# Weight splits in halves and a planner that holds pieces back: one change to an attention and two-mixture kernel

## The chip, the cores and the metric

The kernel runs on one core of a Trainium2 chip. The core has five engines that work side by side, each through its own queue, in the order of the program: TensorE (PE, with PEld for its weight loads), VectorE (DVE), ScalarE (ACT), GpSimd (POOL) and SyncE (SP), which issues most DMAs. The metric is the time of one execution on the device in microseconds; less is better. Three runs of the kernel before took 769.09, 770.85 and 771.26 us, median 770.85.

## The reference

Three layers follow each other: an attention with decaying state, a mixture of four experts in which every token goes through all of them, and a mixture of eight experts in which each token goes to one.

```python
# attention: chunks of tokens, L = decay between two tokens of a chunk, state carried over
y = ((C @ B.T) * L * causal) @ x + (C @ state) * decay_to_i
state = decay_full * state + sum_j(B_j x_j * decay_from_j)
# first mixture: N = 3072 tokens, D = 256, F = 1024, four experts
out = sum_e p[:, e] * (relu(x @ w1[e]) @ w2[e])
# second mixture: eight experts, each token to the argmax of x @ w_gate, times its softmax weight
out[i] = gate_w[i] * (relu(x[i] @ w1[e_i]) @ w2[e_i])
```

## The kernel before

**Numbers in two parts.** The matmuls take their operands in a reduced form of float32, and precision is kept by splitting every operand into a high part (a copy, on ScalarE) and a low part (the subtraction of the two, on VectorE or GpSimd). One product is then three matmuls: high by high, high by low, low by high (lines 533 to 535 for the first layer of an expert, 562 to 564 for the second). `split_w` (line 402) does this for a quarter of an expert's weights: 128 partitions by 1024 columns. A quarter is called a chunk `c`: 0 and 1 make up `w1`, 2 and 3 `w2`.

**Blocks.** The 3072 tokens are 24 steps of 128. The first mixture goes through them in seven blocks of 2, 3, 4, 4, 4, 4 and 3 steps; a matmul of block 0 has 256 columns, of block 1 384, of blocks 2 to 5 512. In each block each expert has eight slices `f` of its hidden layer. `up(b, e, f)` is a group of six matmuls into a PSUM tile `ph`, after which ScalarE writes `hh` = relu (line 538) and VectorE `hl`, the low part (line 539). `down(b, e, f)` is six matmuls from `hh` and `hl` into the accumulators `acc`. `down` runs two slices behind `up` (LAG = 2), so PE's order is `up f`, `down f-2`, `up f+1`, `down f-1` and so on. There are two `ph` buffers: `up f+2` needs `hl` of `f` to be done. There are three buffers for accumulators, and an expert uses two; after its last slice, `combine` multiplies them by the token's weight on VectorE (lines 578 and 583). The opening expert of block 0 (expert 0) is different: its raw weights are multiplied in full float32, one step of 128 tokens after the other (lines 516 and 552, `ph32`), since its weights are not split yet.

**Attention beside it.** While PE goes through a block of the first mixture, the attention of the next block's steps is put in between, in pieces. Per step: `decay` (two scans on VectorE, 128 x 512, tile `lt`, line 181), `prefix` (a scan `pre` and the product `cd`), `low` and `high` (packing of keys and queries into `bp` and `cbd`, lines 206 and 202), `scores` (PE, tiles `sc`, in PSUM), `mask` (two multiplications `m0` and `m1` on VectorE, line 247, `sc` by `lt`), `state_in` (`bw`), `products` (PE: `y` from the state, line 255; the new state, line 291; `y` from the masked scores, line 263: the first half of it reads `m0`, the second `m1`), then `split` (ScalarE's `xh`, VectorE's `xl`) and `state`. The PSUM tiles `sc` and `y` share three buffers: `y` of heads 4 to 7 takes the buffer of `sc0`, and so needs `m0` to be done. `USUAL` and `FIRST` (lines 318 and 321) list which pieces stand together.

**What sets the order.** The order on all engines is that in which the program issues the instructions. `tick` (line 998) is called once after each `up` and once after each `down`; its calls are counted as slots. A slot issues first what a table `wq` has for it (weight splits, loads), then a piece of the routing of the block before, then as many attention pieces as keep them spread evenly over the block. The table at lines 969 to 973 sets the slots in which VectorE splits the first mixture's weights: those of experts 1, 2 and 3 in block 0, and of expert 0 in block 1. Each such split is one ScalarE copy (line 408) and one VectorE subtraction of 1024 columns (line 409). The second mixture's preparation (`part_split`, line 372) has its subtractions already in halves.

Of the kernel before, what the change touches and what calls it, by code (L numbers as in the profile page):

```python
# [17 lines left out]
P = 128  # L18
# [7 lines left out]
FF = 1024  # L26
NF = FF // P
# [9 lines left out]
BLOCKS = [2, 3, 4, 4, 4, 4, 3]  # L37
# [32 lines left out]
def attention_moe_moe_kernel(ctx: ExitStack, tc: tile.TileContext, aps: dict, cap: int):  # L70
    nc = tc.nc
# [90 lines left out]
    def attention_pieces(s, xH, xL, col):  # L162
# [238 lines left out]

    def split_w(moe, e, c, lo):
        if (moe, e) not in W:
            W[moe, e] = weights(moe, e)
        h, l = W[moe, e][2 * (c // 2):2 * (c // 2) + 2]
        sl = slice(FF * (c % 2), FF * (c % 2) + FF)
        st = given[moe, e, c]
        nc.scalar.copy(h[:, sl], st)
        lo.tensor_tensor(l[:, sl], st, h[:, sl].bitcast(F32), ALU.subtract)
# [71 lines left out]
    def block_attention(b):  # L481
        new_xT(b)
        r = []
        for i in range(BLOCKS[b]):
            d = attention_pieces(starts[b] + i, *xT[b], P * i)
            for group in FIRST if starts[b] + i < OPENING else USUAL:
                r.append(lambda fns=[d[k[:-1]][int(k[-1])] for k in group]: [fn() for fn in fns])
        return r

    hid, acc, pb = {}, {}, {}  # L490
# [450 lines left out]
    urgent, side, done = [], [], 0  # L941
    fills = fill_pieces()
    wq = {}

    def at_slot(b, i, fn):
        wq.setdefault((b, i), []).append(fn)

# [21 lines left out]
    for b, i, e, c in (  # L969
# [3 lines left out]
        at_slot(b, i, lambda e=e, c=c: split_w(1, e, c, nc.vector))  # L973
    for i, e, c in ((19, 2, 0), (20, 2, 1), (21, 2, 2), (22, 2, 3), (30, 3, 0), (31, 3, 1), (36, 3, 2), (37, 3, 3)):
# [3 lines left out]
    for i in range(len(apart)):  # L978
        b, s = 2 + i // 3, 16 * (i % 3)
        at_slot(b, s + 2, lambda i=i: part_load(i))  # L980
        at_slot(b, s + 20, lambda i=i: part_split(i, 0))
        at_slot(b, s + 24, lambda i=i: part_split(i, 1))
        at_slot(b, s + 27, lambda i=i: part_store(i))
# [11 lines left out]

    slot = 0

    def tick(b):
        nonlocal slot, done
        nslot = 2 * sum(v[0] == b for v in seq)  # L1000
        for fn in wq.get((b, slot), []):
            fn()
        if b == 1 and fills and slot % 3 == 2:
            fills.pop(0)()
        if b == 1 and slot == nslot - 1:
            while fills:
                fills.pop(0)()
        if urgent:
            urgent.pop(0)()
        wait = 11 if b == 0 else 4  # L1010
        while done < len(side) and done < math.ceil((slot + 1 - wait) * len(side) / (nslot - 6 - wait)):
            side[done]()
            done += 1
        slot += 1

    for i in range(len(seq) + LAG):
        if i < len(seq):
            b, e, f = seq[i]
            if e == experts(b)[0] and f == 0:
                while done < len(side):  # L1020
                    side[done]()
                    done += 1
# [3 lines left out]
                side = block_attention(b + 1) if b + 1 < len(BLOCKS) else []  # L1026
                done, slot = 0, 0
            up(b, e, f)
            tick(b)
        if i >= LAG:  # L1030
# [193 lines left out]
```

## Time and profile before

| | |
|---|---|
| time, median of three runs | 770.85 us |
| the profiled execution | 771.84 us |
| its span, first to last instruction | 770.1 us |
| TensorE | 759.5 us busy, 4746 matmuls |
| VectorE | 444.6 us busy, 892 instructions |
| ScalarE | 286.3 us busy, 589 instructions |
| GpSimd | 159.3 us busy |
| TensorE's granted clock | 0.998 of full speed |

How to read it: matmuls overlap in the record, so that TensorE can be counted busy through a short wait. A wait is seen better as a step between the starts of two matmuls that is longer than others of the same shape. On VectorE and ScalarE too an instruction starts a little before the end of the one in front of it, so that what it costs the queue is the step to the next start, and what a reader of its result waits for is its end.

Times in the profile count from the start of the span. Block 0 lasts from about 14 to 75 us, block 1 from there to about 150 us.

### The profile page before, as it was taken

The page shows a single profiled execution, that of the slowest core. Times are in us where ns is not written, and L with a number is a line of the kernel's source. Part 1 is how long each engine was busy: PE and PEld are TensorE (multiplying, and loading weights), DVE is VectorE, ACT ScalarE, POOL GpSimd, SP SyncE. Part 2 cuts the span into 40 slices and gives each one's busy share as a digit, 9 for nine tenths or more (in the row PEclk, how much of TensorE's full clock was granted, in tenths as well). Part 3 has the DMA queues.
Part 4 walks back from the last instruction along what each step waited for, and adds up shares of the span by engine and source line. Part 5 has one row for each costly group of instructions (what it writes and reads, how often), then busy time and mean ns, then how long its engine had stood idle before and what let it go on. Part 6 is the DMA issues. An engine that isn't in the chain of part 4 may idle for free. (4 is left out here: it accounts for less than half of the span.)

```text
span 770.1 us, 12919 instructions
## 1 busy us (share of the span) xinstructions
PE 759.5 (99%) x4746; PEld 666.5 (87%) x4746; DVE 444.6 (58%) x892; ACT 286.3 (37%) x589; POOL 159.3 (21%) x217
## 2 busy tenths in 40 slices
PE   9999999999999999999999999999999999999996
PEld 7899999988887888878888888888999999999996
DVE  5786778467663686636766356563343444556432
ACT  1552443233332333323333233222345334545432
POOL 1010102212210222101221023110286411111211
PEclk9999999999999999999999999999999999999999
DMA  9763567832433325333253312403053324667100
GB/s 255 233 209 110 186 197 223 231 111 86 162 127 124 113 78 176 127 123 110 80 174 127 123 59 69 142 14 134 15 188 124 93 68 180 233 208 256 56 25 29
DMA packets 55957, 103.50 MB, mean 134 GB/s; under 512 B 5745, under 2 KB 35650, under 8 KB 55869
## 3 DMA queue, kind: packets, MB, share of 16 engines
q1 hardware_dynamic: 52100, 95.48, 38.5%
q0 software_dynamic: 2400, 6.11, 2.2%
q10 hardware_dynamic: 1368, 0.81, 0.5%
q8 instruction: 47, 0.77, 0.4%
q14 instruction: 42, 0.34, 0.1%
HBM read 76.05 MB, written 26.80 MB: 134 GB/s over the span
## 5 line engine op out<-in xcount | busy, mean ns | idle before, releaser
L539 DVE SCALAR_TENSOR_TENSOR hl<-ph,hh 128x512 fp32r<-128x512 f32 (+2 forms) x216 | 133.8, 620 | 220.1 <-ACT hh L538 218.0
L538 ACT ACTIVATE hh<-ph 128x512 fp32r<-128x512 f32 (+2 forms) x216 | 117.4, 543 | 334.0 <-PE ph L535 323.5
L533 PE MATMUL ph<-xh,w1h 128*128 128x512 f32 (+2 forms) x432 | 160.6, 372 | 0.7 <-DVE hl L539 0.7
L562 PE MATMUL acc<-hh,w 128*128 128x512 f32 (+2 forms) x432 | 158.0, 366 | 0.6 <-DVE x L578 0.5
L534 PE MATMUL ph<-xl,w1h 128*128 128x512 f32 (+2 forms) x432 | 156.5, 362 | 0.0
L535 PE MATMUL ph<-xh,w1l 128*128 128x512 f32 (+2 forms) x432 | 156.4, 362 | 0.0
L563 PE MATMUL acc<-hl,w 128*128 128x512 f32 (+2 forms) x432 | 156.3, 362 | 0.0
L564 PE MATMUL acc<-hh,w 128*128 128x512 f32 (+2 forms) x432 | 156.1, 361 | 0.0
L562 PEld LDWEIGHTS acc<-hh,w 128*128 128x128 f32 x432 | 81.2, 188 | 13.0 <-issue 1.4
L533 PEld LDWEIGHTS ph<-xh,w1h 128*128 128x128 f32 x432 | 81.2, 188 | 12.6 <-issue 2.4
L535 PEld LDWEIGHTS ph<-xh,w1l 128*128 128x128 f32 x432 | 81.2, 188 | 10.5
L564 PEld LDWEIGHTS acc<-hh,w 128*128 128x128 f32 x432 | 81.3, 188 | 10.4
L563 PEld LDWEIGHTS acc<-hl,w 128*128 128x128 f32 x432 | 81.3, 188 | 9.4
L534 PEld LDWEIGHTS ph<-xl,w1h 128*128 128x128 f32 x432 | 81.3, 188 | 8.6
L586 POOL TENSOR_TENSOR x<-x,cmb 128x512 f32<-128x512 f32 (+2 forms) x40 | 48.5, 1233 | 150.0 <-DVE cmb L583 150.0
L778 PE MATMUL yy<-w,ring_hh 128*128 128x512 f32 x208 | 76.3, 398 | 0.0
L767 DVE SCALAR_TENSOR_TENSOR ring_hl<-qh,ring_hh 128x384 fp32r<-128x384 f32 (+2 forms) x77 | 36.5, 477 | 55.6 <-ACT ring_hh L766 52.2
L766 ACT ACTIVATE ring_hh<-qh 128x384 fp32r<-128x384 f32 (+2 forms) x77 | 33.0, 428 | 72.2 <-PE qh L764 67.7
L779 PE MATMUL yy<-w,ring_hl 128*128 128x256 f32 x208 | 58.3, 280 | 0.0
L181 DVE TENSOR_TENSOR_SCAN lt<-abc,id 128x512 f32<-128x512 f32 x44 | 56.6, 1287 | 0.0
L778 PEld LDWEIGHTS yy<-w,ring_hh 128*128 128x128 f32 x208 | 39.1, 188 | 6.1
L809 POOL DMA_INDIRECT out<-yo,gi x26 | 25.5, 979 | 78.6 <-DVE yo L808 75.1
(173 smaller groups left out, 991.8 us busy)
## 6 DMA issues: line engine op xcount, KB each, us to landing
stg<-in_w SPq DMA_DIRECT2D x24, 512.0 KB, 3.6
abc<-a_zero SPq DMA_DIRECT2D x21, 512.0 KB, 4.4
bcr<-in_bc SPq DMA_DIRECT2D x19, 512.0 KB, 3.7
disp<-zrow SPq DMA_DIRECT2D x12, 516.0 KB, 8.2
nat<-in_nat SPq DMA_DIRECT2D x24, 256.0 KB, 4.1
raw<-in_w SPq DMA_DIRECT2D x10, 512.0 KB
parts<-high SPq DMA_DIRECT2D x10, 512.0 KB, 3.5
parts<-raw SPq DMA_DIRECT2D x10, 512.0 KB, 3.5
```

Source lines behind the costliest of these rows:

```text
L181: nc.vector.tensor_tensor_scan(t["lt"][:, sl, :].rearrange("p h i -> p (h i)"), a_bc[:, sl, :].rearrange("p h i -> p (h i)"), id4.rearrang ...
L533: nc.tensor.matmul(ph[:, :n], lhsT=wh[:, c], rhs=xh[:, k, :n], start=k == 0, stop=False)
L534: nc.tensor.matmul(ph[:, :n], lhsT=wh[:, c], rhs=xl[:, k, :n], start=False, stop=False)
L535: nc.tensor.matmul(ph[:, :n], lhsT=wl[:, c], rhs=xh[:, k, :n], start=False, stop=k == KD - 1)
L538: nc.scalar.activation(hh[:, :n], ph[:, :n], AF.Relu)
L539: nc.vector.scalar_tensor_tensor(hl[:, :n], ph[:, :n], 0.0, hh[:, :n].bitcast(F32), ALU.max, ALU.subtract)
L562: nc.tensor.matmul(a[:, :n], lhsT=wh[:, c], rhs=hh[:, :n], start=f == 0, stop=False)
L563: nc.tensor.matmul(a[:, :n], lhsT=wh[:, c], rhs=hl[:, :n], start=False, stop=False)
L564: nc.tensor.matmul(a[:, :n], lhsT=wl[:, c], rhs=hh[:, :n], start=False, stop=f == NF - 1)
L586: (nc.vector if (b, e) == (last, experts(b)[-1]) else nc.gpsimd).tensor_tensor(dst[d], dst[d], tmp[d], ALU.add)
L778: nc.tensor.matmul(y, lhsT=hh[:, q], rhs=w2[:, :, c], start=j == 0, stop=False)
L779: nc.tensor.matmul(y[:, 0], lhsT=hl[:, q], rhs=w2[:, 0, c], start=False, stop=j == NF - 1)
```

## The change

A split of a first-mixture chunk on VectorE becomes two instructions of 512 columns, one in each of two slots that follow each other; ScalarE's copy stays whole and goes with the first. The slots are moved: some chunks of experts 1 to 3 come one to eight slots later. And `tick` keeps an estimate `queue` of VectorE's outstanding work, in ns, which falls by `span` with each slot and rises by the load of what is issued. An attention piece with a load in the table `LOAD` (scans, masks, low packs, `state_in`, and the casts and the state update at the end) is held back while the estimate would pass 1.6 slots, until it is three pieces behind its turn (one in the last quarter of a block). Pieces with no load, `scores` and `products` among them, are not held themselves, but they wait for those in front of them in the list. Two helper functions are new: `columns`, the estimate of an instruction, and the changed `at_slot`, which takes a load.

```diff
+    LOAD = dict(
+        prefix0=640, decay0=1280, decay1=1280, low0=640, low1=640, low2=640, mask0=640, mask1=640, state_in0=320,
+        split1=512, state0=448)
...
-    def split_w(moe, e, c, lo):
+    def split_w(moe, e, c, lo, part=None):
...
-        nc.scalar.copy(h[:, sl], st)
+        if part != 1:
+            nc.scalar.copy(h[:, sl], st)
+        if part is not None:
+            half = slice(FF // 2 * part, FF // 2 * part + FF // 2)
+            h, l, st = h[:, sl][:, half], l[:, sl][:, half], st[:, half]
+            sl = slice(None)
         lo.tensor_tensor(l[:, sl], st, h[:, sl].bitcast(F32), ALU.subtract)
...
+    def columns(n):
+        return n * 5 // 4 + 96
...
-            (0, 13, 1, 0), (0, 16, 1, 1), (0, 20, 1, 2), (0, 24, 1, 3), (0, 34, 2, 0), (0, 37, 2, 1), (0, 41, 2, 2),
+            (0, 13, 1, 0), (0, 16, 1, 1), (0, 21, 1, 2), (0, 28, 1, 3), (0, 34, 2, 0), (0, 37, 2, 1), (0, 43, 2, 2),
...
-        at_slot(b, i, lambda e=e, c=c: split_w(1, e, c, nc.vector))
+        for part in range(2):
+            at_slot(b, i + part, lambda e=e, c=c, part=part: split_w(1, e, c, nc.vector, part), columns(FF // 2))
...
+        span = 6 * columns(P * BLOCKS[b]) // 3 if slot >= 4 * NF or b else columns(2 * P)
+        queue = max(0, queue - span) + own
+        for load, fn in wq.get((b, slot), []):
+            queue += load
             fn()
...
-        while done < len(side) and done < math.ceil((slot + 1 - wait) * len(side) / (nslot - 6 - wait)):
-            side[done]()
+        while done < len(side):
+            ahead_of = (slot + 1 - wait) * len(side) / (nslot - 6 - wait) - done
+            load = side[done][0]
+            if ahead_of <= 0 or ahead_of < (3 if 4 * slot < 3 * nslot else 1) and load and queue + load > 8 * span // 5:
+                break
+            queue += load
+            side[done][1]()
             done += 1
...
-            tick(b)
+            tick(b, columns(P * BLOCKS[b]) if (b, e) != (0, 0) else 0)
```

How it moves instructions is shown at three places; names carry the step or the block, expert and slice (`m02` is mask 0 of step 2, `hl0_1_0` the low part of block 0, expert 1, slice 0, `w2_1_1` the split `w2` of expert 1).

VectorE's queue before, from the first scan of step 2 to the first `hl` of expert 1, while the opening expert ends:

```order
L181 SCALAR_TENSOR_TENSOR lt2_338<-abc2_137,id4_87 128x512
L409 TENSOR_TENSOR w1l_1_1_344<-early_w1l_106,w1h_1_1_343 128x1024 x2
L181 SCALAR_TENSOR_TENSOR lt2_338<-abc2_137,id4_87 128x512
L282 TENSOR_TENSOR bw2_389<-nat2_216,lt2_338 128x128
L409 TENSOR_TENSOR w2_1_1_345<-early_w2_104,w2_1_1_345 128x1024
L247 TENSOR_TENSOR m02_402<-sc2_0_362,lt2_338 128x512
L247 TENSOR_TENSOR m12_412<-sc2_1_363,lt2_338 128x512
L409 TENSOR_TENSOR w2_1_1_345<-early_w2_104,w2_1_1_345 128x1024
L936 TENSOR_TENSOR xl0_100<-spare0_101,xh0_99 128x2x256
L539 SCALAR_TENSOR_TENSOR hl0_1_0_474<-ph0_1_0_466,hh0_1_0_473 128x256
```

The same stretch of VectorE's queue after the change:

```order
L417 TENSOR_TENSOR w1l_1_1_342<-early_w1l_106,w1h_1_1_341 128x512 x4
L181 SCALAR_TENSOR_TENSOR lt2_364<-abc2_137,id4_87 128x512
L417 TENSOR_TENSOR w2_1_1_343<-early_w2_104,w2_1_1_343 128x512
L181 SCALAR_TENSOR_TENSOR lt2_364<-abc2_137,id4_87 128x512
L417 TENSOR_TENSOR w2_1_1_343<-early_w2_104,w2_1_1_343 128x512
L282 TENSOR_TENSOR bw2_416<-nat2_216,lt2_364 128x128
L949 TENSOR_TENSOR xl0_100<-spare0_101,xh0_99 128x2x256
L247 TENSOR_TENSOR m02_429<-sc2_0_385,lt2_364 128x512
L417 TENSOR_TENSOR w2_1_1_343<-early_w2_104,w2_1_1_343 128x512
L247 TENSOR_TENSOR m12_445<-sc2_1_386,lt2_364 128x512
L417 TENSOR_TENSOR w2_1_1_343<-early_w2_104,w2_1_1_343 128x512
L552 SCALAR_TENSOR_TENSOR hl0_1_0_478<-ph0_1_0_470,hh0_1_0_477 128x256
```

The masks `m02` and `m12` stood in front of the last chunk's split and of `xl0`; now `xl0`, which needs a cast by ScalarE, stands in front of both, and a half of the last chunk in front of `m12`. On PE the products of step 2 come two groups of four matmul records later (after `ph32_1_7`, before after `ph32_1_6`).

VectorE's queue before, around the masks of step 3, while expert 1 of block 0 ends:

```order
L282 TENSOR_TENSOR bw3_605<-nat3_384,lt3_510 128x128
L409 TENSOR_TENSOR w2_1_2_525<-spare3_103,w2_1_2_525 128x1024
L539 SCALAR_TENSOR_TENSOR hl0_1_6_623<-ph0_1_6_615,hh0_1_6_622 128x256
L247 TENSOR_TENSOR m03_629<-sc3_0_559,lt3_510 128x512
L539 SCALAR_TENSOR_TENSOR hl0_1_7_645<-ph0_1_7_637,hh0_1_7_644 128x256
L247 TENSOR_TENSOR m13_648<-sc3_1_560,lt3_510 128x512
L409 TENSOR_TENSOR w2_1_2_525<-spare3_103,w2_1_2_525 128x1024
L539 SCALAR_TENSOR_TENSOR hl0_2_0_666<-ph0_2_0_658,hh0_2_0_665 128x256
L539 SCALAR_TENSOR_TENSOR hl0_2_1_701<-ph0_2_1_693,hh0_2_1_700 128x256
L583 TENSOR_TENSOR cmb0_1_0_710<-acc0_1_0_528,pb0_1_477 128x256
L583 TENSOR_TENSOR cmb0_1_1_712<-acc0_1_1_529,pb0_1_477 128x256
```

The same stretch after the change:

```order
L417 TENSOR_TENSOR w2_1_2_516<-spare3_103,w2_1_2_516 128x512
L282 TENSOR_TENSOR bw3_657<-nat3_400,lt3_574 128x128
L552 SCALAR_TENSOR_TENSOR hl0_2_0_667<-ph0_2_0_659,hh0_2_0_666 128x256
L417 TENSOR_TENSOR w2_1_2_516<-spare3_103,w2_1_2_516 128x512
L247 TENSOR_TENSOR m03_678<-sc3_0_613,lt3_574 128x512
L552 SCALAR_TENSOR_TENSOR hl0_2_1_688<-ph0_2_1_680,hh0_2_1_687 128x256
L417 TENSOR_TENSOR w2_1_2_516<-spare3_103,w2_1_2_516 128x512
L596 TENSOR_TENSOR cmb0_1_0_698<-acc0_1_0_519,pb0_1_481 128x256
L596 TENSOR_TENSOR cmb0_1_1_700<-acc0_1_1_520,pb0_1_481 128x256
L247 TENSOR_TENSOR m13_704<-sc3_1_614,lt3_574 128x512
L552 SCALAR_TENSOR_TENSOR hl0_2_2_734<-ph0_2_2_726,hh0_2_2_733 128x256
```

Both masks stood in front of the second split of `w2_1_2` and of the two combines `cmb`; now `m13` is behind both halves of it and both combines.

PE's queue before, around the products of step 3:

```order
L562 MATMUL acc0_1_1_529<-hh0_1_6_622,w2_1_1_345 128x256
L563 MATMUL acc0_1_1_529<-hl0_1_6_623,w2_1_1_345 128x256
L564 MATMUL acc0_1_1_529<-hh0_1_6_622,w2_1_1_345 128x256
L255 MATMUL y3_0_675<-cd3_501,state_85 64x128 x2
L255 MATMUL y3_1_676<-cd3_501,state_85 64x128 x2
L291 MATMUL y3_1_676<-nat3_384,bw3_605 32x64 x4
L263 MATMUL y3_0_675<-m03_629,nat3_384 32x128 x4
L263 MATMUL y3_1_676<-m13_648,nat3_384 32x128 x4
L533 MATMUL ph0_2_1_693<-xh0_99,w1h_1_2_523 128x256
```

PE's queue after the change, at the same products:

```order
L575 MATMUL acc0_1_1_520<-hh0_1_7_646,w2_1_1_343 128x256
L576 MATMUL acc0_1_1_520<-hl0_1_7_647,w2_1_1_343 128x256
L577 MATMUL acc0_1_1_520<-hh0_1_7_646,w2_1_1_343 128x256
L255 MATMUL y3_0_706<-cd3_558,state_85 64x128 x2
L255 MATMUL y3_1_707<-cd3_558,state_85 64x128 x2
L291 MATMUL y3_1_707<-nat3_400,bw3_657 32x64 x4
L263 MATMUL y3_0_706<-m03_678,nat3_400 32x128 x4
L263 MATMUL y3_1_707<-m13_704,nat3_400 32x128 x4
L546 MATMUL ph0_2_2_726<-xh0_99,w1h_1_2_514 128x256
```

The products, which read `m13` last, follow slice 7 of expert 1's `down` (before slice 6), which is what the combines read, with no group between.

VectorE's queue before, around mask 1 of step 6 in block 1:

```order
L539 SCALAR_TENSOR_TENSOR hl1_2_4_1409<-ph1_2_4_1401,hh1_2_4_1408 128x384
L247 TENSOR_TENSOR m06_1412<-sc6_0_1398,lt6_1389 128x512
L181 SCALAR_TENSOR_TENSOR lt6_1389<-abc6_1214,id4_87 128x512
L539 SCALAR_TENSOR_TENSOR hl1_2_5_1436<-ph1_2_5_1428,hh1_2_5_1435 128x384
L247 TENSOR_TENSOR m16_1446<-sc6_1_1423,lt6_1389 128x512
L539 SCALAR_TENSOR_TENSOR hl1_2_6_1456<-ph1_2_6_1448,hh1_2_6_1455 128x384
```

The same stretch after the change:

```order
L552 SCALAR_TENSOR_TENSOR hl1_2_4_1418<-ph1_2_4_1410,hh1_2_4_1417 128x384
L181 SCALAR_TENSOR_TENSOR lt6_1421<-abc6_1255,id4_87 128x512
L247 TENSOR_TENSOR m06_1432<-sc6_0_1423,lt6_1421 128x512
L552 SCALAR_TENSOR_TENSOR hl1_2_5_1442<-ph1_2_5_1434,hh1_2_5_1441 128x384
L181 SCALAR_TENSOR_TENSOR lt6_1421<-abc6_1255,id4_87 128x512
L552 SCALAR_TENSOR_TENSOR hl1_2_6_1468<-ph1_2_6_1460,hh1_2_6_1467 128x384
L247 TENSOR_TENSOR m16_1471<-sc6_1_1455,lt6_1421 128x512
```

`m16` stood in front of `hl1_2_6` and now stands behind it. PE's `up` of slice 6, which `hl1_2_6` reads, comes right before the products of step 6 in both kernels.

From block 2 on the order of PE differs only in that the second scores of steps 12, 16 and 20 come one `down` later, and that of VectorE in single low packs and scans that move by an instruction or a few.

## Rows read from the trace of the kernel before

**Rows 1.** The page's first part: busy time of each engine, share, instructions.

```profile
PE 759.5 (99%) x4746; PEld 666.5 (87%) x4746; DVE 444.6 (58%) x892; ACT 286.3 (37%) x589; POOL 159.3 (21%) x217
```

**Rows 2.** View of waits, PE: engine, line, releaser, us in total, times, longest.

```profile
PE ph L533 <- DVE hl L539: 0.7, 2, 0.4
```

**Rows 3.** Timeline, PE, steps at the waits: start, us, what, [idle before, releaser].

```profile
36.68 0.28 PE L563 MATMUL acc<-hl,w 128*128 128x256 f32 x1
36.80 0.28 PE L564 MATMUL acc<-hh,w 128*128 128x256 f32 x1
37.57 0.38 PE L562 MATMUL acc<-hh,w 128*128 128x256 f32 x1 [0.49 <-DVE x L578]
37.79 0.28 PE L563 MATMUL acc<-hl,w 128*128 128x256 f32 x1
...
56.76 0.28 PE L564 MATMUL acc<-hh,w 128*128 128x256 f32 x1
57.47 0.39 PE L533 MATMUL ph<-xh,w1h 128*128 128x256 f32 x1 [0.43 <-DVE hl L539]
...
101.48 0.33 PE L563 MATMUL acc<-hl,w 128*128 128x384 f32 x1
101.66 0.34 PE L564 MATMUL acc<-hh,w 128*128 128x384 f32 x1
102.22 0.47 PE L229 MATMUL sc<-cbd,bp 128*128 128x256 f32 x2 [0.23 <-DVE cbd L206]
```

**Rows 4.** Timeline, PE, around the products of step 2.

```profile
29.44 0.61 PE L552 MATMUL acc<-h,early_w1h 128*128 128x128 f32 x4
29.89 0.61 PE L516 MATMUL ph<-spare,stg 128*128 128x128 f32 x4
30.43 0.43 PE L255 MATMUL y<-cd,state 32*64 32x128 f32 x4
31.04 0.43 PE L255 MATMUL y<-cd,state 32*64 32x128 f32 x4 [0.18 <-DVE m L247]
...
31.54 0.62 PE L263 MATMUL y<-m,nat 128*32 128x128 f32 x16
32.09 0.71 PE L552 MATMUL acc<-h,early_w1h 128*128 128x128 f32 x4
...
34.24 0.61 PE L552 MATMUL acc<-h,early_w1h 128*128 128x128 f32 x4
```

**Rows 5.** Timeline, DVE, the same stretch.

```profile
30.30 1.28 DVE L247 TENSOR_TENSOR m<-sc,lt 128x512 f32<-128x512 f32 x2
31.50 1.21 DVE L409 TENSOR_TENSOR w<-early_w,w 128x1024 fp32r<-128x1024 f32 x1
32.63 0.68 DVE L936 TENSOR_TENSOR xl<-spare,xh 128x512 fp32r<-128x512 f32 x1
34.92 0.42 DVE L539 SCALAR_TENSOR_TENSOR hl<-ph,hh 128x256 fp32r<-128x256 f32 x1 [1.60 <-ACT hh L538]
35.26 0.48 DVE L275 TENSOR_TENSOR xl<-y,xh 128x128 fp32r<-128x128 f32 x2
...
36.10 0.42 DVE L539 SCALAR_TENSOR_TENSOR hl<-ph,hh 128x256 fp32r<-128x256 f32 x1
```

**Rows 6.** Timeline, ACT, the same stretch.

```profile
29.88 1.04 ACT L408 CAST w<-early_w 128x1024 fp32r<-128x1024 f32 x1
...
30.98 0.62 ACT L935 CAST xh<-spare 128x512 fp32r<-128x512 f32 x1
33.34 0.28 ACT L519 ACTIVATE h<-ph 128x128 f32<-128x128 f32 x1 [1.75 <-PE ph L516]
```

**Rows 7.** Timeline, DVE, the first combine of expert 1.

```profile
50.84 0.74 DVE L583 TENSOR_TENSOR cmb<-acc,pb 128x256 f32<-128x256 f32 x2
```

**Rows 8.** Timeline of PE and DVE, the products of step 6.

```profile
108.51 0.62 PE L263 MATMUL y<-m,nat 128*32 128x128 f32 x16
...
109.00 0.56 DVE L539 SCALAR_TENSOR_TENSOR hl<-ph,hh 128x384 fp32r<-128x384 f32 x1 [0.93 <-ACT hh L538]
```

More of the change, by code (lines that the diff above doesn't have):

```diff
@@ L486, in block_attention @@
             for group in FIRST if starts[b] + i < OPENING else USUAL:
-                r.append(lambda fns=[d[k[:-1]][int(k[-1])] for k in group]: [fn() for fn in fns])
-        return r
+                r.append((
+                    sum(LOAD.get(k, 0) for k in group),
+                    lambda fns=[d[k[:-1]][int(k[-1])] for k in group]: [fn() for fn in fns]))
+        return r
+    def columns(n):
+        return n * 5 // 4 + 96
     hid, acc, pb = {}, {}, {}
@@ L943, in attention_moe_moe_kernel, with at_slot @@
     wq = {}
-    def at_slot(b, i, fn):
-        wq.setdefault((b, i), []).append(fn)
+    def at_slot(b, i, fn, load=0):
+        wq.setdefault((b, i), []).append((load, fn))
     def split_at(b, slots, moe, e, engines=(nc.gpsimd,) * 4):
@@ L980, in attention_moe_moe_kernel @@
         at_slot(b, s + 2, lambda i=i: part_load(i))
-        at_slot(b, s + 20, lambda i=i: part_split(i, 0))
-        at_slot(b, s + 24, lambda i=i: part_split(i, 1))
+        at_slot(b, s + 20, lambda i=i: part_split(i, 0), columns(FF // 2))
+        at_slot(b, s + 24, lambda i=i: part_split(i, 1), columns(FF // 2))
         at_slot(b, s + 27, lambda i=i: part_store(i))
@@ L994, in attention_moe_moe_kernel, with tick @@
     at_slot(last, 48, lambda: turned(0, 0))
-    slot = 0
-    def tick(b):
-        nonlocal slot, done
+    slot = queue = 0
+    def tick(b, own=0):
+        nonlocal slot, done, queue
         nslot = 2 * sum(v[0] == b for v in seq)
-        for fn in wq.get((b, slot), []):
+        span = 6 * columns(P * BLOCKS[b]) // 3 if slot >= 4 * NF or b else columns(2 * P)
+        queue = max(0, queue - span) + own
+        for load, fn in wq.get((b, slot), []):
+            queue += load
             fn()
@@ L1020, in attention_moe_moe_kernel @@
                 while done < len(side):
-                    side[done]()
+                    side[done][1]()
                     done += 1
@@ L1039, in attention_moe_moe_kernel @@
             if i < len(seq):
-                tick(b)
+                tick(b, 2 * columns(P * BLOCKS[bb]) if ff == NF - 1 else 0)
     ahead = [(0, k) for k in range(1, min(nblk, 2))] + [(1, 0)]
```

2 rows, old and new, of the table steps1 are left out of this document.

## Prediction, made before the changed kernel was run

> **What bounds the kernel now.** I read the page's first part first: TensorE (PE) is counted busy for 759.5 of 770.1 us, VectorE (DVE) for 444.6 [rows 1]. A busy PE hides short waits, because matmuls overlap in the record, so I then read the view of waits for PE and the timeline of PE where it names VectorE. The reader is to see two things. First, the step from one matmul to the next is regular (0.12 us for 256 columns, 0.18 for 384 [rows 3]), and exceptions are few. Second, the view of waits charges PE little to VectorE (0.7 us in two waits to the `hl` subtractions [rows 2]), and the rows of these waits lie where VectorE also splits the first mixture's weights [rows 3]. The time is therefore PE's work plus PE's waits. PE's work is not changed, so every microsecond of this change is a wait removed or added on PE.
>
> The waits that can go [rows 3]: from 36.80 to 37.57 PE stood for 0.77 - 0.12 = 0.65 us behind the combine of the opening expert, and the step after it took 0.22 in place of 0.12, since the next weights had not been loaded ahead; 0.75 in all. At 56.76 it was 0.71 - 0.12 = 0.59 and 0.10 again, 0.7; there is a second wait of this kind (both together are 0.7 in the view of waits [rows 2]), which I take at 0.45. At 101.66 it was 0.56 - 0.18 = 0.4 behind the low half of `cbd`, and 0.1 after it. Sum 2.4 us. This is all that the change can win from the waits it reorders; other short ones keep their order.
>
> **The change part by part.** *Halves.* 16 subtractions of 1024 columns become 32 of 512. A whole one goes on after 1.13 us (31.50 to 32.63); one of 512 columns of the same kind takes 0.68 and two in a row go on every 0.60 [rows 5]. So each split costs VectorE 2 x 0.60 - 1.13 = 0.07 us more, 1.1 us in all, beside an engine that is idle four tenths of the time: nothing by itself. The ScalarE copy in front is not halved: 1.04 us [rows 6], and the first half waits for all of it.
>
> *Held pieces.* The estimate delays scans, masks and low packs by up to three pieces, but the products have no load in the table, so they go as soon as their turn comes, now close behind the masks. What PE waits for is then decided by what stands in front of the mask in VectorE's queue. I follow the queue at the places that the order shows.
>
> Step 2 (third chunk, during the opening expert). The products stand two groups later on PE: `ph32_1_6` starts at 29.89, each group takes 0.45 (29.44 to 29.89), so PE is there at 29.89 + 3 x 0.45 = 31.25, about 31.3 [rows 4]. On VectorE mask 0 now stands behind `xl0`, which needs ScalarE's cast, done at 30.98 + 0.62 = 31.6 [rows 6]. So `xl0` at 31.6, mask 0 from 32.2 to 32.9. The second half of the state product, which takes mask 0's PSUM buffer, would come 0.61 - 0.18 = 0.43 after the first (30.43 to 31.04, less the wait in the row's bracket), at 31.75, and waits until 32.95: 1.2 us. In front of mask 1 stands a half of the last weight chunk; its ScalarE copy now comes after the last Relu (0.28), so it ends at 31.6 + 0.28 + 1.04 = 32.9, the half at 33.5, mask 1 at 34.2. The weighted products' second half would come at 32.95 + 0.50 + 0.28 = 33.75 (31.04 to 31.54, and half of 31.54 to 32.09) and waits 0.5. Together 1.7 us; before, the same place waited 0.18 [rows 4]. Net +1.5. Behind mask 1 on VectorE are a half and the first `hl`, which wait for PE anyway. Bounds: +1.1, if the copy overlaps so that only `xl0` holds PE, and +2.0.
>
> The combine's wait then goes: it no longer stands behind the casts, the state update and the scan of the next step. -0.75.
>
> The sixth `up` of expert 1 (`ph0_1_5`) must wait until `hl0_1_3` has read its PSUM buffer. With u the end of `ph0_1_2`: `hl0_1_2` starts at u + 0.68 (34.24 to 34.92 [rows 4, 5]), ScalarE's copy ends at u + 1.7, two halves at 2.9, the casts and the state at 2.9 + 0.84 (35.26 to 36.10) = 3.75, `hl0_1_3` at 4.2. PE has five groups of 6 x 0.12 = 0.72 before it, 3.6, because the scores that stood between are moved away. Wait 0.6, and 0.1 after it: +0.7. Bounds 0.3 and 1.1, by when ScalarE starts the copy.
>
> Step 3. With u the end of `ph0_2_0`: ScalarE's copy of the last chunk ends at u + 1.7, its first half at 2.3, mask 0 at 2.95. PE is at the products after three groups, 2.16 + 0.1, and at the second half of the state product, 0.43 on, at 2.7: waits 0.3. It would be at mask 1 at 3.0 + 0.78 = 3.8. VectorE meanwhile goes on from 2.9 with `hl0_2_1` (0.34), the second half (0.60), the two combines (0.74 [rows 7]), and ends mask 1 (0.68) at 5.2. Wait 1.4. Sum +1.7. The combines read what PE ends just ahead of the products, and the half (0.60) and `hl` (0.34) alone are 0.9 in front of them: bounds 0.9 and 2.4.
>
> The two waits on `hl` (1.15) go: halves stand alternately with `hl`, 0.94 us in a period of 1.44.
>
> Block 1. The low `cbd` of step 6 has a whole `up` group more: -0.5. But step 6's mask 1 now stands behind `hl1_2_6`, which needs the `up` group right in front of the products on PE. Before, this `hl` started at 109.00 as soon as it could; it goes on after about 0.48 of its 0.56, so mask 1 is done at 109.5 + 0.68 = 110.2, where PE was at 108.51 + 0.28 = 108.8 [rows 8]. Wait 1.4, and no luck in the queue can shorten it: bounds 1.3 and 1.6. In step 5 the same flip has one down group more (6 x 0.18 = 1.05): 0.2, between 0 and 0.4.
>
> Blocks 2 to 4. Low packs of steps 10, 14 and 18 move behind an `hl` and a half split, still a full group ahead of their scores: 0.3 for all, between 0 and 0.8 (one 0.60 too late and a little). SP's queue: step 3's decay load goes behind three weight loads, but its scan too stands some 6 us later; nothing.
>
> **Sum.** +1.5 - 0.75 + 0.7 + 1.7 - 1.15 - 0.5 + 1.4 + 0.2 + 0.3 = +3.4 us. The profiled execution took 771.84 us (span 770.1 and 1.7 around it), so 775.2; it lay 1.0 above the median of the runs, 770.85, so I forecast 774.3.
>
> **The rivals.** *B, the waits that it was made for go and nothing comes in their place*: 771.84 - 2.4 = 769.4, against the median 768.45, -0.31%, faster. It decides wherever masks are done before PE arrives, that is if VectorE's queue ahead of them is at most one `hl`. For it: VectorE is idle four tenths of the time and PE's waits are all on it. [...] Against it: step 6's mask cannot start before an `hl` that did not start before 109.00, whatever the queue.
>
> *C, the new waits come at their lower ends*: 1.1 + 0.3 + 0.9 + 1.3 - 2.4 = +1.2, 772.05 against the median, within 0.3%. For it: each PE wait also gives VectorE and ScalarE time to catch up, so a later wait shrinks by part of an earlier one; I let only the waits on the combine and on `hl` profit. Against it: in steps 2, 3 and 6 the queue in front of the mask hangs on PE's own last group, and moves with it.
>
> *D, the stalls cascade*: PE's delay in block 0 puts off everything on ScalarE too, and a late copy holds later `hl`s: upper ends, 2.0 + 1.1 + 2.4 + 1.6 + 0.4 + 0.8 - 2.0 = +6.3, 777.15. For it: ScalarE's copies stay whole and in line with the Relus. Against it: behind step 3's products VectorE has room in each period, 0.94 of 1.44.
>
> *E, the change doesn't do what it says* (the hold never acts): the order excludes it.
>
> **How the numbers follow.** About 0.3%, 2.3 us, is what a measurement of this kernel can tell from no change. Forecast (+2.3 to +5.0) 0.56, D 0.1, C (-2.3 to +2.3) 0.24, B 0.1. Slower 0.66, same 0.24, faster 0.1. The range goes from 770.8, which leaves B and the lowest part of C out, to 777.0: 0.8 of the chance. The forecast's own range is 773.2 to 775.9.
>
> **What would show it.** In the profile after: PE's view of waits names the masks (`m`, the line of the mask's multiplication) several times with waits over 0.5 us, with PE standing at about 31.7 and in the products of steps 3 and 6; the waits on the combine at 37 us and on `hl` at 57 us are gone; PE's times after 150 us are those of before, moved by a constant. Step 6 is the surest: if PE does not wait over a microsecond for `m` there, my reading of the order is wrong. If PE reaches the end of block 0 (the first 384-column `up`) no later than before, the terms of steps 2 and 3 were wrong, and the forecast with them.

## The result and the profile after

The changed kernel took 777.0 us (median of 6 runs, 775.86 to 778.15) against 770.82 us of the kernel before (6 runs, 769.09 to 771.26): the ratio is 1.0082, with a 95% interval of 1.0068 to 1.0096. It is slower by 6.2 us where 3.4 were forecast: 777.0 is the upper end of the range, and +6.2 is just past the +6.15 (777.0 less 770.85) that the range allowed. The profiled execution took 775.86 us, span 774.1.

The first part of the page after, TensorE's (PE's) line. Its busy time is still 759.5 us [rows 1]; the span is 4.0 us longer:

```profile
PE 759.5 (98%) x4746; PEld 666.1 (86%) x4746; DVE 446.1 (58%) x908; ACT 286.6 (37%) x589; POOL 157.2 (20%) x217
```

The view of waits of PE, after (us in total, times, longest). It answers to [rows 2]: the masks `m` take 4.2 us where they took 0.4, POOL's product `bw` appears, and one wait on `hl` is left, at another place:

```profile
PE y L263 <- DVE m L247: 2.5, 4, 1.2
PE y L255 <- DVE m L247: 1.7, 3, 1.0
...
PE y L291 <- POOL bw L282: 0.8, 2, 0.6
PE ph L546 <- DVE hl L552: 0.7, 1, 0.7
...
PE sc L229 <- DVE cbd L206: 0.2, 1, 0.2
```

The masks in the same view before:

```profile
PE y L263 <- DVE m L247: 0.2, 1, 0.2
PE y L255 <- DVE m L247: 0.2, 1, 0.2
```

PE's timeline after (start, us, line, operation; the bracket is the idle time before and what ended it), at the products of step 2, the sixth `up` of expert 1, the products of steps 3 and 5, and the products of step 6:

```profile
30.74 0.43 PE L255 MATMUL y<-cd,state 32*64 32x128 f32 x4
32.18 0.43 PE L255 MATMUL y<-cd,state 32*64 32x128 f32 x4 [1.00 <-DVE m L247]
...
33.50 0.43 PE L263 MATMUL y<-m,nat 128*32 128x128 f32 x8 [0.42 <-DVE m L247]
...
40.97 0.28 PE L577 MATMUL acc<-hh,w 128*128 128x256 f32 x1
41.93 0.39 PE L546 MATMUL ph<-xh,w1h 128*128 128x256 f32 x1 [0.68 <-DVE hl L552]
...
51.49 0.43 PE L255 MATMUL y<-cd,state 32*64 32x128 f32 x4 [0.31 <-DVE m L247]
...
53.59 0.43 PE L263 MATMUL y<-m,nat 128*32 128x128 f32 x8 [1.20 <-DVE m L247]
...
95.11 0.43 PE L255 MATMUL y<-cd,state 32*64 32x128 f32 x4 [0.37 <-DVE m L247]
...
111.26 0.32 PE L291 MATMUL y<-nat,bw 128*32 128x64 f32 x8 [0.58 <-POOL bw L282]
...
112.46 0.43 PE L263 MATMUL y<-m,nat 128*32 128x128 f32 x8 [0.66 <-DVE m L247]
```

VectorE's timeline after, at the same places. At step 2, mask 0 (31.44) stands behind `xl0`, mask 1 (32.76) behind a half. At 39.40 two halves and the casts stand ahead of the `hl` at 41.46. At step 3, mask 1 (52.85) stands behind a half and two combines. At step 6, the second scan (109.45) and then an `hl` stand ahead of mask 1 (111.72):

```profile
30.83 0.69 DVE L949 TENSOR_TENSOR xl<-spare,xh 128x512 fp32r<-128x512 f32 x1 [0.40 <-ACT xh L948]
31.44 0.69 DVE L247 TENSOR_TENSOR m<-sc,lt 128x512 f32<-128x512 f32 x1
32.15 0.69 DVE L417 TENSOR_TENSOR w<-early_w,w 128x512 fp32r<-128x512 f32 x1
32.76 0.68 DVE L247 TENSOR_TENSOR m<-sc,lt 128x512 f32<-128x512 f32 x1
...
39.40 1.29 DVE L417 TENSOR_TENSOR w1l<-early_w,w1h 128x512 fp32r<-128x512 f32 x2 [0.51 <-ACT w1h L412]
40.61 0.48 DVE L275 TENSOR_TENSOR xl<-y,xh 128x128 fp32r<-128x128 f32 x2
...
41.46 0.42 DVE L552 SCALAR_TENSOR_TENSOR hl<-ph,hh 128x256 fp32r<-128x256 f32 x1
...
51.59 0.68 DVE L417 TENSOR_TENSOR w<-spare,w 128x512 fp32r<-128x512 f32 x1
52.18 0.75 DVE L596 TENSOR_TENSOR cmb<-acc,pb 128x256 f32<-128x256 f32 x2
52.85 0.69 DVE L247 TENSOR_TENSOR m<-sc,lt 128x512 f32<-128x512 f32 x1
...
109.45 1.22 DVE L181 TENSOR_TENSOR_SCAN lt<-abc,id 128x512 f32<-128x512 f32 x1
111.25 0.56 DVE L552 SCALAR_TENSOR_TENSOR hl<-ph,hh 128x384 fp32r<-128x384 f32 x1 [0.58 <-ACT hh L551]
111.72 0.68 DVE L247 TENSOR_TENSOR m<-sc,lt 128x512 f32<-128x512 f32 x1
```

The two profiles are compared best from PE's first product on, since the start before it differs from execution to execution (two profiles of the changed kernel have that product at 13.77 and 14.65 us). PE's timeline of the kernel before: the first product of the opening expert, the first `up` matmul with 384 columns (the end of block 0 on PE) and the last one:

```profile
14.35 1.16 PE L516 MATMUL ph<-spare,stg 128*128 128x128 f32 x8 [0.17 <-ACT spare L188]
...
74.52 0.34 PE L533 MATMUL ph<-xh,w1h 128*128 128x384 f32 x1
...
601.00 0.33 PE L533 MATMUL ph<-xh,w1h 128*128 128x384 f32 x1
```

The same three of the changed kernel:

```profile
13.77 1.16 PE L529 MATMUL ph<-spare,stg 128*128 128x128 f32 x8 [0.17 <-ACT spare L188]
...
76.70 0.34 PE L546 MATMUL ph<-xh,w1h 128*128 128x384 f32 x1
...
605.49 0.33 PE L546 MATMUL ph<-xh,w1h 128*128 128x384 f32 x1
```

Block 0 took 74.52 - 14.35 = 60.17 us and takes 76.70 - 13.77 = 62.93, +2.76. From there to the last `up` it took 526.48 and takes 528.79, +2.31. Together the change adds 5.07 us of waiting; the changed profile happened to start 0.58 earlier and to be 0.46 shorter behind the last `up`, which leaves the 4.0 between the profiles.

### The profile page after: what moved, and what is told of

Same layout as the page of the kernel before. It is cut to its first block, busy times and chain, and to the rows that moved or that the text cites. A ratio compares the mean times of both kernels' runs of the same rounds, so it can differ in the third digit from the quotient of the medians.

```text
span 774.1 us, 12941 instructions
## 1 busy us (share of the span) xinstructions
PE 759.5 (98%) x4746; PEld 666.1 (86%) x4746; DVE 446.1 (58%) x908; ACT 286.6 (37%) x589; POOL 157.2 (20%) x217
## 5 line engine op out<-in xcount | busy, mean ns | idle before, releaser
L599 POOL TENSOR_TENSOR x<-x,cmb 128x512 f32<-128x512 f32 (+2 forms) x40 | 44.8, 1142 | 170.0 <-DVE cmb L596 169.9
L780 DVE SCALAR_TENSOR_TENSOR ring_hl<-qh,ring_hh 128x384 fp32r<-128x384 f32 (+2 forms) x77 | 36.8, 477 | 56.6 <-ACT ring_hh L779 55.5
L181 DVE TENSOR_TENSOR_SCAN lt<-abc,id 128x512 f32<-128x512 f32 x44 | 54.6, 1240 | 0.0
```

The lines of the kernel that those rows point to most:

```text
L181: nc.vector.tensor_tensor_scan(t["lt"][:, sl, :].rearrange("p h i -> p (h i)"), a_bc[:, sl, :].rearrange("p h i -> p (h i)"), id4.rearrang ...
L599: (nc.vector if (b, e) == (last, experts(b)[-1]) else nc.gpsimd).tensor_tensor(dst[d], dst[d], tmp[d], ALU.add)
```

## The experiments

"Slots" are the calls of `tick`. Each run was timed beside the kernel before, whose median is given with it. The last table puts all profiles side by side.

**Run 1: the changed kernel again.** No edit.

> The changed kernel itself once more, to see what of the 6 us between the medians is in the program. Theory of the added waits (the mask waits and what follows them are all of it): 4.5 to 5 us over the kernel before when the two traces are counted from the first product of the opening expert on, and every profile of the changed kernel shows the same waits; the rest of the 6 us is the first 14 us, where the profiled execution of the changed kernel happened to be 0.6 us early. Rival (a second cost, later in the program): another execution of the changed kernel shows a wait of 1 us or more behind 40 us that the first profile does not have.

Measured: 776.72 us against 771.68, ratio 1.0075 (1.0057 to 1.0094). The execution that was profiled took 779.51, and all mask waits stand in it as in the first profile. Its 3.65 us over the first profile lie nearly all in three places: 0.88 ahead of the first product (14.65 against 13.77), 1.51 in block 0, and 1.16 behind the last `up`, where the trace shows one matmul of the second mixture 0.9 us late, at 704.55 us. That late matmul is not the change's: the profiles of runs 2, 3, 4 and 12 show it too. The 1.51 in block 0 do not come from longer waits. The windows of run 1 just behind the waits of step 2 (busy times, then the granted clock, DMA share and GB/s) show PE busy at a granted clock of 0.50:

```profile
34.00:35.00 1.00, 0.61 (x9) 0.23 (x9) 0.93 (x2) 0.27 (x1) 0.00 (x0) 0.68 0.75 151
35.00:36.00 1.00, 1.00 (x9) 1.00 (x6) 0.00 (x0) 0.27 (x1) 0.00 (x0) 0.50 1.11 221
36.00:37.00 1.00, 1.00 (x6) 1.00 (x6) 0.00 (x0) 0.00 (x0) 0.00 (x0) 0.50 0.96 229
37.00:38.00 1.00, 1.00 (x8) 1.00 (x7) 0.01 (x1) 0.38 (x1) 0.00 (x0) 0.62 1.03 309
```

The same stretch in the first profile of the same program:

```profile
35.00:36.00 1.00, 1.00 (x11) 1.00 (x10) 0.20 (x1) 0.38 (x1) 0.00 (x0) 1.00 1.03 295
36.00:37.00 1.00, 1.00 (x11) 1.00 (x10) 0.26 (x2) 0.38 (x1) 0.00 (x0) 1.00 1.10 303
```

At 0.50 the step from one matmul of 256 columns to the next was 0.21 us (36.21 to 36.42 in run 1), at 1.00 it was 0.12 (35.81 to 35.93 in the first profile). Ahead of this stretch PE stood 1.00 and 0.42 us for the two masks of step 2, in both profiles. So the first theory holds for the waits, and there is a further cost that it had no term for: in some executions the clock falls behind them, here to 0.50.

**Run 2: halves, nothing held back.**

```diff
-            if ahead_of <= 0 or ahead_of < (3 if ...) and load and queue + load > 8 * span // 5:
+            if ahead_of <= 0:
```

> The halves at their new places stay; nothing is held back, so pieces of attention go at the slots they had before. Theory (holding back makes the waits, halves are nearly free): 769 to 771 us; no wait for a mask over 0.3 us in steps 2, 3 and 6; the waits for the hl subtractions at 55 and 57 us smaller than before. Rival (the halves are the cost: twice the instructions, the last part of each chunk later): 774 to 777 us, with waits on hl or on the weights in block 0.

Measured: 771.84 us against 771.68, ratio 1.0005 (0.9991 to 1.0020). The median lies just above the 769 to 771 that was expected, and it is that of the kernel before within its interval: the halves and their new places cost nothing and win nothing that can be measured. The two waits on `hl` at 55 and 57 us are gone from the trace, but the combine's wait at 36 us is 1.0 us over the usual step, a new one on an `hl` at 34.9 us is 0.4, and one on a mask of step 2 is 0.56, more than the 0.3 expected. Holding back makes the loss. In this trace the halves ended two waits, lengthened another and made new ones, with no gain in time.

**Run 3: holding back, whole splits at the old places.**

```diff
-        for part in range(2):
-            at_slot(b, i + part, lambda ...: split_w(1, e, c, nc.vector, part), columns(FF // 2))
+        at_slot(b, i, lambda e=e, c=c: split_w(1, e, c, nc.vector), columns(FF))
```

The table of slots goes back with it.

> Whole splits at the places of before, with the holding back kept (its estimate of the queue gets the load of a whole split). Theory (holding back makes the waits): 774 to 777 us, the mask waits of steps 2, 3 and 6 as in the changed kernel: over 1 us for step 6, over 1 us for step 2. Rival (halves are the cost): 769 to 772 us.

Measured: 776.73 us against 771.68, ratio 1.0066 (1.0045 to 1.0087). Step 2's second half of the state product stands 1.9 us for its mask, step 6 0.6 for `bw` and 0.6 for mask 1. PE's granted clock is 0.50 from 34 to 40 us. Holding back alone is as slow as the whole change.

**Run 4: masks not held back.**

```diff
-        prefix0=640, ..., mask0=640, mask1=640, state_in0=320,
+        prefix0=640, ..., state_in0=320,
```

> The changed kernel, but the masks carry no load: a mask goes when its turn comes, the scans, decays and low packs are still held back. Theory (a mask that is held back stands right in front of its products): the wait of step 2 falls from 1.9 to under 1 us; that of step 3 from 2.0 to under 0.8; step 6 keeps 1.3 or more, since its scores still stand a group later. In all 2 to 3 us less than the changed kernel: 773.5 to 775. Rival (it is the queue itself, not the mask's place): no more than 0.7 us less than the changed kernel.

Measured: 773.56 us against 771.68, ratio 1.0029 (1.0015 to 1.0044): 3 us less than the changed kernel. Step 2 keeps one wait of 0.8, step 3 none. Step 6 keeps 0.6 for `bw` and loses the one for mask 1, which I had expected to stay: in this order mask 1 stands ahead of the `hl`.

**Runs 5 to 7: no holding back in one stretch each.** The edit is one more condition on the same line:

```diff
-... and load and queue + load > 8 * span // 5:
+... and load and not (b == 0 and slot < 36) and queue + ...     # run 5: opening
+... and load and not (b == 0 and slot >= 36) and queue + ...    # run 6: rest of block 0
+... and load and b != 1 and queue + ...                         # run 7: block 1
```

> The changed kernel; in the first 36 slots (opening expert and the start of the next: step 2) nothing is held back, the rest as changed. Theory (waits of this stretch as counted on TensorE): the waits of step 2 (1.3 + 0.7) and the one on hl0_1_3 (0.8) go, and the waits that the order without holding had there come back (0.6 + 0.4 + 1.0): 0.8 us less. And with the clock: in two of three profiles with these waits TensorE's granted clock stood at 0.5 to 0.6 from about 34 us on for 3 to 6 us, costing 1.6 to 3; without the waits it stays at 1.00. So 774 to 776 us by the median, and a profile with 1.00 at 34 to 40 us. Rival (the clock falls by itself in some executions, whatever the waits): a profile with a low clock here too, and only 0.8 us less.

> The changed kernel; nothing is held back from slot 36 of block 0 to its end (steps 3 and 4). Theory: the two mask waits of step 3 (0.57 + 1.47) go, about 0.2 comes back: 1.8 us less than the changed kernel, 774.5 to 775.5 by the median; step 2's waits and those of steps 5 to 7 as in the changed kernel. Rival (step 3's loss comes back later in block 0, since the halves need the place): 0.5 us less or nothing.

> The changed kernel; nothing is held back in block 1 (steps 5 to 8). Theory: waits of step 5 (0.63), step 6 (0.74 on the weighted state and 0.92 on mask 1) and step 7 (0.26) go, the wait on the low cbd (0.4 to 0.7) comes back: 1.5 to 2 us less than the changed kernel, 774.5 to 775.5 by the median. Step 2's waits stay, so the granted clock may fall behind them. Rival (these waits are given back by TensorE's next wait): under 0.7 us less.

Measured against 770.94: 775.13 (ratio 1.0056, 1.0040 to 1.0071), 775.82 (1.0059, 1.0038 to 1.0081) and 774.45 (1.0047, 1.0030 to 1.0064). Run 5 lies in the range expected, run 6 0.3 us above its own and run 7 just below. The traces tell more than the medians. Run 5: block 0 takes 61.99 us in place of 62.93, -0.94, at full clock. Run 6: the mask waits of step 3 are gone, and so is the one on `hl0_1_3`, though the scores of step 3 now wait 0.72 us at 40.93; block 0 takes 63.01 all the same, since PE's granted clock is low from 42 to 47 us, which by its windows of 1 us costs an estimated 0.13 + 3 x 0.50 + 0.08 = 1.7. Less that, 61.3: -1.6. Run 7: the stretch behind block 0 takes 526.90 in place of 528.79, -1.9. The three sum to 4.4 of the 5.07 (run 6 by the estimate of its clock): the stretches add up, and each loses by its own order.

**Run 8: the products kept apart from the masks.** Everything is held back as in the change; the products go at the earliest three slots behind the second mask.

```diff
+            if side[done][1] == ["products0"] and slot - masked < 3 and 8 * slot < 7 * nslot:
+                break
...
+            if "mask1" in side[done][1]:
+                masked = slot
```

> The changed kernel, held pieces and halves as they are, but the products of a step go at the earliest three slots behind its second mask. Theory (held masks cost because their products follow at once): no wait for a mask over 0.3 us in steps 2, 3, 5 and 6, that is 5.5 to 6 us less wait; new waits of up to 2 us (the next step's state is later): 771 to 773 us, against about 777. Rival (the queue itself is the cost): the waits move to the next thing that reads VectorE's output; 775 to 777.

Measured: 771.17 us against 770.94, ratio 1.000 (0.9988 to 1.0011). 5 us are back. The view of waits of run 8 has no row on `m`; what comes in its place is named there:

```profile
PE sc L229 <- DVE cbd L206: 1.1, 2, 0.9
...
PE acc L575 <- DVE cmb L596: 0.8, 1, 0.8
PE ph L546 <- DVE hl L552: 0.7, 1, 0.7
```

The masks stand where they stood in the changed kernel, as late and behind the same instructions (up to 240 us VectorE's order differs only in where a few `xl`, halves, `hl` and `cbd` stand); only PE asks for them later. Mask 1 of step 3 and the products that read it, in run 8:

```profile
52.28 0.68 DVE L247 TENSOR_TENSOR m<-sc,lt 128x512 f32<-128x512 f32 x1
...
53.87 0.62 PE L263 MATMUL y<-m,nat 128*32 128x128 f32 x16
```

The mask ends at 52.96, ahead of the products. So it is the distance from mask to product that made the loss.

**Run 9: ScalarE's copies halved too.** This tests rival D of the prediction.

```diff
-        if part != 1:
-            nc.scalar.copy(h[:, sl], st)
         if part is not None:
             half = slice(FF // 2 * part, FF // 2 * part + FF // 2)
             ...
+        nc.scalar.copy(h[:, sl], st)
```

> The changed kernel with ScalarE's copy of a weight chunk halved too: each half of 512 columns is copied right before its subtraction. Theory D of the prediction (whole copies make the subtractions behind them late): the first half is ready some 0.4 us sooner, so the wait on mask 1 of step 2 falls from 0.7 to 0.2, the one on hl0_1_3 from 0.8 to 0.4, the first one of step 3 from 0.6 to 0.2: 1.2 to 1.5 us less. Theory of the order (what stands in front of the masks decides, not the copy): at most 0.5 us less, the second wait of step 3 (1.47, behind the combines) and those of step 6 as before. By the median 775.5 to 776.5.

Measured: 775.96 us against 771.43, ratio 1.0062 (1.0048 to 1.0077). PE's timeline of run 9 shows the sixth `up` of expert 1 (41.19) without a bracket: its step from the matmul before is 0.19 us where it was 0.96.

```profile
41.00 0.28 PE L576 MATMUL acc<-hh,w 128*128 128x256 f32 x1
41.19 0.39 PE L545 MATMUL ph<-xh,w1h 128*128 128x256 f32 x1
```

The whole copy was the cause of that wait, and the first wait of step 3 went too (0.57 to 0.12 over the usual step). Mask 1 of step 2 fell only from 0.68 to 0.56, and the wait of 1.47 stands unchanged: there D does not hold. The waits that went sum to 0.94 + 0.45 + 0.12 = 1.5 us, what was expected by D and more than the 0.5 that the order's theory allowed; so some 1.5 of the 5.07 hang on the whole copies, and the rest does not. In the profiled execution the clock then fell behind the wait of 1.47, and block 0 took 63.12 us where it took 62.93 with whole copies (windows of run 9):

```profile
53.00:54.00 1.00, 1.00 (x7) 1.00 (x7) 0.00 (x0) 0.17 (x1) 0.00 (x0) 0.59 0.28 83
54.00:55.00 1.00, 1.00 (x7) 1.00 (x7) 0.42 (x1) 0.85 (x2) 0.00 (x0) 0.50 0.14 43
55.00:56.00 1.00, 1.00 (x6) 1.00 (x6) 0.69 (x1) 0.04 (x1) 0.00 (x0) 0.50 0.00 0
```

**Run 10: held back and kept apart in the opening stretch alone.** As run 8, with `b == 0 and slot < 36` on the hold and `b == 0 and slot < 40` on the distance.

> Halves at the changed places; pieces held back only in the opening stretch of block 0 (first 36 slots), with the products there at least three slots behind the second mask; nothing is held back or kept apart elsewhere. Theory (the stretches add up: each stretch's waits are those that its own order makes): the wait on hl0_1_3 (0.8) stays, the combine's of 51 us (0.9), the cbd waits of 118 us (1.05 against some 0.5) and 185 us (0.4) of the kernel with all products apart are gone: 1.7 us less than it, and 1 to 1.5 less than the kernel before, 769 to 770 us. Rival (the stretches do not add up, what one wins another gives back): the time of the kernel before within 0.5 us.

Measured: 771.74 us against 771.43, ratio 1.0006 (0.9994 to 1.0017): a miss. The combine's wait of 51 us and the cbd waits went as expected, but a combine's of 0.5 us stands at 118.6 as in run 2; the scores of step 3, which now stand early, waited 0.71 us (at 39.78) for `xl`, the low part of step 2's output, which stands behind two halves and reads a tile `y`, of the buffers that `sc` and `y` share; and a wait on an `hl` stayed, 0.75 over the usual step. It is the rival that came true.

**Run 11: the same, with two chunks of the third expert later.**

```diff
-            ... (0, 34, 2, 0), (0, 37, 2, 1), (0, 43, 2, 2),
+            ... (0, 36, 2, 0), (0, 40, 2, 1), (0, 44, 2, 2),
```

> As the one with the opening stretch alone, and the splits of the third expert's first two chunks three and two slots later (36 and 40 in place of 34 and 37), so that the state's casts stand ahead of them on VectorE. Theory: the wait on hl0_1_3 (0.8) goes too: 768.2 to 769.2 us, faster than the kernel before by 1.7 to 2.5. Rival (the weights of the third expert are then too late): a new wait of 0.5 us or more at its first product, about 46 us, and no gain.

Measured: 771.00 us against 771.43, ratio 0.9995 (0.9983 to 1.0007): a miss again. The scores no longer wait, but two scans and a half now stand ahead of another `hl`, and PE stands 1.10 us for it at 44.06.

**Run 12: halves of copies and subtractions, and holding back with distance in the first 40 slots alone.** The edits of runs 9 and 10 together, with the limit of 40 in both conditions.

> What the runs so far point to, in one kernel: halves at the changed places with ScalarE's copies halved too; pieces held back only in the first 40 slots of block 0, the products there at least three slots behind the second mask; nothing held back later. Theory (the waits at each place are those that its own order makes): left are the wait on the cast of the input (0.45 at 32 us), 0.25 at 52 us, 0.67 at 117 us; the combine's at 37 us and those on hl0_1_3 and on masks are gone, and the granted clock stays at 1.00: 769 to 770.3 us, 1 to 2 less than the kernel before. Rival (each wait removed in the opening stretch turns into a later one there, as in the two kernels before this): 771 to 772, the same as the kernel before.

Measured: 770.31 us against 771.83, ratio 0.9976 (0.9962 to 0.9990): 1.5 us less than the kernel before, and the only version whose interval lies below 1. That is 0.2%, less than the 0.3% which the prediction took as the least that can be told, but the trace agrees with it: block 0 is 1.14 us shorter than before, and the stretch to the last `up` 0.54. The view of waits of run 12, without the rows of the first 14 us:

```profile
PE qh L774 <- DVE ring_hl L779: 0.8, 1, 0.8
...
PE acc L574 <- DVE cmb L595: 0.3, 1, 0.3
PE ph L546 <- DVE xl L948: 0.2, 1, 0.2
PE y L263 <- DVE m L247: 0.2, 1, 0.2
```

The first row is the late matmul near 700 us; the others are the longest waits left in the attention and the first mixture.

All profiles, counted as above from PE's first product (us); "rest" goes from the last `up` to the start of PE's last matmul:

| profile | block 0 | to the last `up` | rest | clock under 0.97 between 14 and 134 us |
|---|---|---|---|---|
| before | 60.17 | 526.48 | 162.32 | none |
| changed | 62.93 | 528.79 | 161.86 | none |
| 1, changed again | 64.44 | 528.82 | 163.02 | 34 to 38 |
| 2, halves, no hold | 61.00 | 526.34 | 163.04 | none |
| 3, hold, whole splits | 66.14 | 527.46 | 163.07 | 33 to 41 |
| 4, masks not held | 61.68 | 526.81 | 163.10 | none |
| 5, opening free | 61.99 | 528.86 | 161.91 | none |
| 6, rest of block 0 free | 63.01 | 528.91 | 161.86 | 42 to 47 |
| 7, block 1 free | 64.43 | 526.90 | 161.79 | 34 to 38 |
| 8, products apart | 60.22 | 526.60 | 161.80 | none |
| 9, copies halved | 63.12 | 528.62 | 161.73 | 53 to 57 |
| 10, opening alone | 60.79 | 526.41 | 161.86 | none |
| 11, and slots | 60.10 | 526.42 | 161.87 | none |
| 12, together | 59.03 | 525.94 | 163.09 | none |

Runs 2 and 4 began their first product about 2 us earlier than the others (12.4 and 12.3 us), and run 2 then waited 0.4 us for its first weights, which is in its block 0.

## Why the prediction was wrong in size

The direction, the bound (PE's waits) and the mechanism (masks held back close ahead of products that are not) were right: run 2 clears the halves, run 3 convicts the holding back, and run 8 gives the 5 us back by distance alone. Rival B is out, since PE does arrive ahead of the masks, and rival C, since 5.07 us of wait are added. Too small was the sum: the waits alone pass the +5.0 at which the forecast's own range ends.

What each term measured, from step to step of PE's matmuls, less the usual step and less the same place before:

| term | forecast | measured |
|---|---|---|
| products of step 2 | +1.5 | 1.27 + 0.68 - 0.44 = +1.5 |
| combine at 36.8 | -0.75 | -0.75 |
| sixth `up` of expert 1 | +0.7 | 0.84 + 0.10 = +0.9 |
| products of step 3 | +1.7 | 0.42 + 1.47 = +1.9 |
| two waits on `hl` | -1.15 | -1.1 |
| cbd of step 6 | -0.5 | -0.6 |
| products of step 6 | +1.4 | 0.65 (`bw`) + 0.92 (mask 1) = +1.6 |
| step 5 | +0.2 | +0.5 |
| step 7 | none | +0.3 |
| low packs (step 10) | +0.3 | +0.4 |
| a combine at 121.6 | none | +0.1 |

The measured terms sum to 4.8 of the 5.07; the forecast's sum was 3.4. No term has the wrong sign; seven of the eleven were taken 0.1 to 0.3 too low or left out, and none too low by more. The step of the working that failed is the one on block 1, "Block 1. The low `cbd` of step 6 ...": it forecast +1.1 there, and with step 7 and the combine it is +1.9. The 0.8 are 0.3 in step 5 (its term was 0.2, though its own working, 1.4 less 1.05, gives 0.35), 0.3 in step 7, 0.2 in step 6 and 0.1 at the combine, less 0.1 at `cbd`. It followed the mask alone. The held second scan also feeds POOL's `bw`, and PE needs `bw` before it needs mask 1. The row of POOL's timeline after:

```profile
110.80 0.41 POOL L282 TENSOR_TENSOR bw<-nat,lt 128x128 f32<-128x128 f32 x1 [16.99 <-PE ph L548]
```

Its bracket names a matmul, but the scan (109.45 + 1.22 = 110.67) ended within 0.02 us of it, and the same 0.14 us lie between scan and product before (105.67 + 1.21 to 107.02), where the product, of 0.41 us, ended 0.94 us ahead of PE's need at 108.37. Now PE stood 0.58 us for it, so only 0.66 were left to wait for the mask. My own test, a wait over a microsecond for `m` in step 6, was not met for that reason, while the whole wait there, 1.6, was near the 1.4 forecast. So in step 6 `bw` only shares the wait; in step 7 PE stands 0.26 for `bw`, which had no term at all.

The second thing that failed is silent in every step: each wait was priced at its own length, with PE's clock taken as full behind it. Runs 1, 3, 6, 7 and 9 show granted clocks of 0.50 for 3 to 7 us behind waits, at an estimated 1.7 us (run 1, from its windows: 0.32 + 0.50 + 0.50 + 0.38, of which its block 0 shows 1.5) or, in run 3, about 3.4. The profile of the kernel before had none (1.00 in every window of 4 us from 14 to 758 us), and so no row to take a price from.

How much of the 6.2 between the first medians is the clock is not settled. The waits alone put the changed kernel at 770.82 + 5.07 = 775.9, where three of its six runs lie (775.86 to 776.17). The other three, 777.8 to 778.2, have 2 us more, and were not profiled. The mean granted clock of all six is 0.997, which speaks against a low stretch in the slower ones; the start (0.88 in run 1) and the stretch behind the last `up` (1.16) would make 2.0 together. The kernel before has two such groups of its own: of its 23 runs beside run 9 six took 768.3 to 769.8 us and the others 771.0 to 772.3. In the second comparison, run 1, the medians differ by 5.0.

Rival D gave 777.15, nearly the time measured, but only part of it by its mechanism. Run 9 took the whole copies away and with them 1.5 us, the wait on `hl0_1_3` above all, as D says; the waits of 1.27, 1.47 and 0.9 stayed. A forecast by D would have been near for a reason that is mostly wrong.

Right in detail were the queue in front of each mask of step 2 (32.13 for the end of mask 0 on a timeline that starts 0.6 earlier, against 32.9), the place and length of step 3's second wait, and that times after block 1 are moved by a constant, but for the 0.4 of step 10: +5.07 at the last `up`, with the first 2.76 of it made in block 0.

## What to carry to other kernels

A rule that holds back a producer should hold back its consumer by as much: here the scans and masks carried a load and the products did not, so the slack between them, which had cost nothing, was what the rule spent. Before pricing such a rule, list everything that the held instruction feeds on every engine (here the mask, and POOL's product beside it), and price them in the order in which PE reaches them. When a wait of about a microsecond is put on the bounding engine, its price can have a tail (here a clock of 0.50 for some 3 to 7 us in four of the eight profiles with such a wait, at an estimated 1.7 us in run 1 and 3.4 in run 3): look at the granted clock in the windows behind it in more than one profile.

## What the runs showed of the hardware

In five of the fourteen profiles PE's granted clock fell to 0.50 behind waits of 0.7 to 1.9 us. By the brackets of the timelines between 28 and 60 us, PE stood 1.0 us or more at a stretch in eight of the fourteen profiles (the changed kernel twice, runs 3, 5, 6, 7, 9 and 11). In four of them (runs 1, 3, 7 and 9) the granted clock right behind such a wait was 0.50 for some 3 to 7 us, though PE was busy in them; in the other four it stayed at 1.00 there. In run 6 it fell only 10 us later, from 42.7 us, behind a shorter wait:

```profile
40.93 1.15 PE L242 MATMUL sc<-spare 16*128 16x128 f32 x14 [0.72 <-DVE xl L275]
```

Run 10 has the same wait, 0.71 at 39.78, and kept 1.00, as did the other five profiles, with waits of up to 0.84. So the length of a wait alone does not tell whether the clock falls, and what does was not tested. The same program did both: the first profile of the changed kernel kept 1.00 behind the same two waits, run 1 did not. In run 1 the cost was 1.5 us in block 0.

Two differences between executions have nothing to do with the change: PE's first product came between 12.3 and 14.9 us, and the stretch behind the last `up` took either 161.7 to 161.9 us or 163.0 to 163.1, with the kernel before between them at 162.3. Run 1 and the first profile are the same program and lie on either side. The longer one has the late matmul near 700 us, and it went with the chip: runs 1 to 4 on one chip and run 12 on another have it, runs 5 to 11 on two others do not.
